# One fifth of the first MLP layer's matmuls on half the TensorE array

## The chip, the cores and the metric

The kernel runs on one core of one Trainium2 chip. A core has TensorE (PE; its weight loads are listed apart as PEld), VectorE (DVE), ScalarE (ACT), GpSimd (POOL), SyncE (SP, which here issues most transfers) and 16 DMA engines. The metric is the device time of one execution in microseconds (us).

## The reference

The input `x` is 8 batches of 4224 rows of 192 features. A causal convolution over 7 rows with softmaxed taps per head comes first; then the real part of a Fourier transform over rows and features is added, each row is normalised, and a two-layer MLP is added to the row:

```python
def _moe_ref(x, w_ch1, w_ch2) -> np.ndarray:
    X = np.fft.fft(x, axis=1)
    X = np.fft.fft(X, axis=2)
    mixed = np.real(X).astype(np.float32)
    u = x + mixed
    ...
    un = (u - mu) / np.sqrt(var + 1e-06)
    ch = np.maximum(un @ w_ch1, 0.0) @ w_ch2
    return (u + ch).astype(np.float32)
```

`w_ch1` is 192 x 768 and `w_ch2` 768 x 192; `x` there is the output of the convolution.

## The kernel before

A batch goes through nine steps: one of 128 tokens (`it == 0`) and eight of 512, so 72 steps in all. Work of four kinds overlaps.

- **Front of later batches**: the convolution (`conv_part`, on TensorE from tile `xt`, and `conv_tap`, on ScalarE and GpSimd from `xg`), a scratch `sc` in memory, loads of `xs` from it (`load_x`, L484), their split in float16 halves `xh` and `xl`, and the transforms `stage_b` (matmuls into `pb`) and `stage_a` (into `pv`, then `V`).
- **`prep`** of the next two steps: matmuls into `pe` (64 array columns wide in iteration 0, 128 otherwise), the residual `u` with `xr`, the normalised rows `un`, and their float16 halves in `hl`. `transposes` turns `hl` into `kt` with one DMA from SyncE's queue.
- **`mlp_hidden`**: six hidden tiles of 128 units. Every float32 factor is carried as a high and a low float16 half. The 192 features take two blocks of array rows: features 0 to 127 fill one (`kt[:, 0]` high, `kt[:, 2]` low), and for features 128 to 191 both halves lie in one block, `kt[:, 1]`, high on partitions 0 to 63 and low on 64 to 127. The weights `W1[:, 0]` and `W1[:, 1]` are the halves of rows 0 to 127; `W1[:, 2]` and `W1[:, 3]` are those of the last 64 rows, laid on both halves of the partitions. Five matmuls of 512 tokens make a hidden tile in one PSUM bank `ph`; ScalarE takes its ReLU to `hh` and VectorE the remainder to `hlo`.
- **`mlp_out`**: for each group of 128 tokens of the step before, 18 matmuls of 192 columns (L724, L727, L730) into `po`, then VectorE adds to `u`, which is stored.

PSUM has eight banks: four with the tag `f` (transforms, `pe`, convolution), two `h` (hidden tiles) and two `o` (`po`). The code writes the units of these kinds in an interleaved order, but each engine's final order is made by a scheduler when the program is built, from the waits and the buffers. Each engine runs its own order strictly, and so does SyncE's queue.

Of the kernel before, what the change touches and what calls it, by code (L numbers as in the profile page):

```python
# [11 lines left out]
F32 = mybir.dt.float32  # L12
I32 = mybir.dt.int32
U32 = mybir.dt.uint32
AF = mybir.ActivationFunctionType
# [21 lines left out]
# From batch NB0 on, the heads from HP on are convolved by segments of SR rows, one a  # L37
# partition.
# [3 lines left out]
# Powers of two that keep the float16 halves of the transform in range.  # L42
# [52 lines left out]
def token_rows():  # L95
    """Row of the result for each (group, partition) of one batch."""
# [23 lines left out]
def kernel(  # L120
# [22 lines left out]
    # ------------------------------------------------------------ constants  # L143
# [37 lines left out]
    # band[h][i, r] = weight of tap k where i + r = 125 - k: rows of a padded vector  # L181
# [12 lines left out]
    # taps[:, h, i] = weight of tap 6 - i of head h on all partitions  # L194
    taps = cp.tile([128, NH, KS], F32, name="taps")

    def pow2_of_norm(parts, n, exponent, name):
        """2^exponent * 2^floor(log2(1 / norm)) on all partitions, where norm^2 is the
        sum of parts[:, :n] over partitions and columns."""
        tot = sb.tile([128, 1], F32, tag="nrm", name=f"tot_{name}", bufs=8)  # L200
        nc.vector.tensor_reduce(tot, parts[:, :n], axis=AX.X, op=ALU.add)
        tag, bufs = ("h", 2) if name[0] == "w" else ("f", 4)
# [26 lines left out]
        # sign and top exponent bit, 7 low exponent bits, 23 leading mantissa bits  # L229
# [4 lines left out]
        # the 29 mantissa bits below, as a float32, to round to nearest  # L234
# [4 lines left out]
        # zero below float32's normal range  # L239
# [98 lines left out]
    def store_rows(bt, xa, r0, cols):  # L338
        """The rows from r0 on, and the first of all once more after the last."""
# [20 lines left out]
    def conv_chunk(bt, ch, tag, xt_slot, xa_slot):  # L360
        """All heads of WC windows."""
# [9 lines left out]
        for h0 in range(0, NH, 3):  # L371
# [3 lines left out]
                bufs=4 if tag == "f" else 2,  # L375
# [22 lines left out]
    def conv_part(bt, part):  # L398
        """One head of WL windows of the heads that the tensor engine convolves."""
# [8 lines left out]
        pc = ps.tile([128, WL, GRP], F32, tag="f", name=f"pc_{b}_{part}", bufs=4)  # L408
# [37 lines left out]
    def store_segments(bt, part):  # L446
        """A third of each segment, or the first segments once more after the last."""
# [15 lines left out]
    # ------------------------------------------------------ transform over b and d3  # L463
    def load_x(bt, ch):
# [6 lines left out]
        # Row 33 a + 128 b of the doubled rows below b1, that less 4224 from there.  # L471
# [31 lines left out]
    def stage_b(bt, t):  # L503
# [6 lines left out]
        pb = ps.tile([128, 512], F32, tag="f", name=f"pb_{b}_{t}", bufs=4)  # L510
# [14 lines left out]
    # -------------------------------------------------------------- transform over a  # L525
    def stage_a(bt, it):
        """V of the one or two q of iteration it."""
# [5 lines left out]
        for h, q in enumerate(qs):  # L533
            pv = ps.tile([128, ND, 2, 64], F32, tag="f", name=f"pv_{b}_{it}_{h}", bufs=4)
# [13 lines left out]
        # Times i where the sine's place holds the alternating sum.  # L548
# [8 lines left out]
    # ------------------------------------- transform over j, residual, LN, transposes  # L557
# [25 lines left out]
    def prep(bt, it):  # L583
# [5 lines left out]
        pe = ps.tile([128, 2, ND, NC], F32, tag="f", name=f"pe_{b}_{it}", bufs=4)  # L589
# [47 lines left out]
        # 1 / sqrt(var + eps), one Newton step after the square root  # L637
# [12 lines left out]
        for g in range(ng):  # L650
# [28 lines left out]
    # --------------------------------------------------------------------- the MLP  # L679
    anchor = [None]  # L680

    def in_turn():
        """No earlier than the latest hidden tile."""
        return tc.issue_after(anchor[0]) if anchor[0] else ExitStack()

    def hidden_units(it):
        """Hidden tiles that share a bank."""
        return ((0, 1, 2), (3, 4, 5)) if it == 0 else ((0,), (1,), (2,), (3,), (4,), (5,))

    def mlp_hidden(bt, it, hts):  # L690
        b = bt.b
        nt = 128 if it == 0 else 512
# [5 lines left out]
        hh, hlo = (h[:, hts[0] : hts[-1] + 1, :nt] for h in bt.h[it])  # L698
# [308 lines left out]
```

## Time and profile before

| | |
|---|---|
| time, median of 3 runs | 1469.61 us (1466.17 to 1475.82) |
| span of the profiled execution | 1470.0 us |
| mean granted clock of TensorE | 0.917 |
| PE busy | 1200.6 us (82%), 11324 matmuls |
| PEld, DVE, ACT, POOL busy | 927.6, 1008.5, 747.5, 671.4 us |
| DMA | 170.68 MB, mean 116 GB/s |

The page gives the profiled execution's span, not a time of its own; it lies beside the median. Matmuls are pipelined: a row's duration runs to the end of its result, and the next starts long before. So what a matmul costs in a series is the distance between two starts in the timeline.

### The profile page before, as it was taken

The numbers are of one execution on the slowest core, as the hardware profiler recorded it, in microseconds if no ns is written. First come the engines' busy times: TensorE is split into PE (matmuls) and PEld (weight loads), VectorE is DVE, ScalarE is ACT, GpSimd is POOL, SyncE is SP. The second block draws the span as 40 slices with busy tenths as digits, with TensorE's granted clock in tenths as the row PEclk, the third lists the DMA queues.
The fourth block names the chain that finished last, engine by engine and source line by source line (L and its number), as shares of the span: only waits on it lengthen the run. The fifth ranks groups of instructions, "written<-read, shape, count | busy, mean of one in ns | idle before, by whom it ended". The sixth has DMA issues, their size and how long they took to land.

```text
span 1470.0 us, 29177 instructions
## 1 busy us (share of the span) xinstructions
PE 1200.6 (82%) x11324; PEld 927.6 (63%) x11324; DVE 1008.5 (69%) x2410; ACT 747.5 (51%) x1400; POOL 671.4 (46%) x708
## 2 busy tenths in 40 slices
PE   4038947997699958999599986999689994999998
PEld 4038635775568736777367764687467772788766
DVE  5424856877586758867597685967588674867773
ACT  4145645645566446654466455664476442434432
POOL 0022444654476436854277544864278542224410
PEclk9568987999899989999799998999799997999999
DMA  8455734465623746437443656227563454423312
GB/s 256 91 133 159 204 78 98 91 151 151 142 61 70 183 138 126 95 105 195 94 101 94 145 160 145 67 63 183 139 132 94 107 106 77 83 55 86 88 44 54
DMA packets 322561, 170.68 MB, mean 116 GB/s; under 512 B 279616, under 2 KB 304696, under 8 KB 322424
## 3 DMA queue, kind: packets, MB, share of 16 engines
q1 hardware_dynamic: 236832, 115.45, 34.4%
q10 hardware_dynamic: 75992, 33.72, 9.2%
q0 software_dynamic: 9600, 19.67, 4.9%
q8 instruction: 88, 1.44, 0.4%
q14 instruction: 49, 0.40, 0.1%
HBM read 84.35 MB, written 58.49 MB: 97 GB/s over the span
## 4 chain that ended last, share of the span: by engine, by line
PE 44%; DVE 18%; SPq 13%; DMA 12%; ACT 5%; issue 4%; ACTq 2%; POOL 1%; another core or an unknown queue 0%; DVEq 0%; POOLq 0%
PE ph L705 16%; SPq L484 10%; PE po L730 5%; PE po L727 5%; PE po L724 5%; DVE un L651 4%; DMA kt<-hl 3%; DVE hlo L710 3%; DMA xt<-in_xv_dram 3%; PE pb L515 2%; PE pb L516 2%; PE pb L514 2%; DMA xs<-sc 2%; DVE xl L497 2%; PE pc L378 2%
## 5 line engine op out<-in xcount | busy, mean ns | idle before, releaser
L705 PE MATMUL ph<-kt,W 128*128 128x512 f16 (+1 forms) x2160 | 510.8, 371 | 91.2 <-DMA kt<-hl 53.9
L709 ACT ACTIVATE hh<-ph 128x512 f16<-128x512 f32 (+1 forms) x400 | 236.3, 591 | 338.8 <-PE ph L705 273.1
L724 PE MATMUL po<-W,hh 128*128 128x192 f16 x1584 | 388.8, 249 | 11.8 <-ACT hh L709 6.1
L710 DVE SCALAR_TENSOR_TENSOR hlo<-ph,hh 128x512 f16<-128x512 f32 (+1 forms) x400 | 269.8, 676 | 182.8 <-ACT hh L709 181.1
L730 PE MATMUL po<-W,hlo 128*128 128x192 f16 x1584 | 386.4, 249 | 3.7 <-DVE hlo L710 3.7
L727 PE MATMUL po<-W,hh 128*128 128x192 f16 x1584 | 388.3, 249 | 0.5 <-issue 0.5
L705 PEld LDWEIGHTS <-W 128*128 128x128 f16 x2160 | 199.1, 101 | 246.0 <-issue 60.0
L569 POOL DMA_INDIRECT xr<-sc,rows_sb x200 | 202.4, 1012 | 284.7 <-DMA rows_sb<-in_rows_dram 96.7
L442 POOL TENSOR_TENSOR pr<-pr,pr 128x792 f32<-128x792 f32 x120 | 233.1, 1943 | 173.6 <-ACT pr L437 168.6
L666 POOL TENSOR_TENSOR hl<-un,hl 128x256 f16<-128x256 f32 (+2 forms) x144 | 128.9, 914 | 155.6 <-ACT hl L664 154.6
L724 PEld LDWEIGHTS <-hh 128*128 128x128 f16 x1584 | 159.7, 101 | 32.1 <-ACT hh L709 8.2
L730 PEld LDWEIGHTS <-hlo 128*128 128x128 f16 x1584 | 157.5, 100 | 34.7 <-DVE hlo L710 4.9
L727 PEld LDWEIGHTS <-hh 128*128 128x128 f16 x1584 | 157.2, 99 | 30.6 <-issue 10.5
L437 ACT ACTIVATE pr<-xg,taps 128x792 f32<-128x792 f32 x168 | 159.2, 959 | 12.1 <-POOL pr L442 11.9
L514 PE MATMUL pb<-c_sb,xh 99*128 99x102 f16 x512 | 127.7, 252 | 3.9 <-ACT xh L494 3.9
L515 PE MATMUL pb<-c_sb,xh 99*128 99x102 f16 x512 | 130.4, 258 | 0.0
L516 PE MATMUL pb<-c_sb,xl 99*128 99x102 f16 x512 | 127.2, 255 | 1.2 <-DVE xl L497 1.2
L497 DVE SCALAR_TENSOR_TENSOR xl<-xs,s_x,xh 99x1024 f16<-99x1024 f32 x64 | 99.8, 1564 | 36.5 <-DMA xs<-sc 28.3
L409 PE MATMUL pc<-xt,band 128*120 128x288 f32 x144 | 52.8, 482 | 70.6 <-DMA xt<-in_xv_dram 70.2
L651 DVE TENSOR_SCALAR un<-u,mv,y 128x192 f32<-128x192 f32 x264 | 103.2, 449 | 9.0 <-POOL hl L666 3.7
L514 PEld LDWEIGHTS <-xh 99*128 99x128 f16 x512 | 103.3, 202 | 7.7 <-ACT xh L494 4.2
L516 PEld LDWEIGHTS <-xl 99*128 99x128 f16 x512 | 105.1, 209 | 2.8 <-DVE xl L497 1.4
(138 smaller groups left out, 2107.4 us busy)
## 6 DMA issues: line engine op xcount, KB each, us to landing
out_dram<-u SPq DMA_DIRECT2D x63, 384.0 KB
sc<-xa ACTq DMA_DIRECT2D x24, 540.0 KB
xg<-in_xg_dram SPq DMA_DIRECT2D x18, 624.0 KB
xt<-in_xv_dram SPq DMA_DIRECT2D x18, 576.0 KB
sc<-xg ACTq DMA_DIRECT2D x18, 528.0 KB
xt<-in_xw_dram SPq DMA_DIRECT2D x12, 576.0 KB
xs<-sc SPq DMA_DIRECT2D x24, 264.0 KB
xr<-sc SPq DMA_DIRECT2D x128, 48.0 KB
```

The costliest lines, as they stand in the source:

```text
L442: nc.gpsimd.tensor_tensor(to, bt.acc, pr, op=ALU.add)
L514: nc.tensor.matmul(po, bt.xh[:, :, j], R[:, 0], start=True, stop=False)
L515: nc.tensor.matmul(po, bt.xh[:, :, j], R[:, 1], start=False, stop=False)
L516: nc.tensor.matmul(po, bt.xl[:, :, j], R[:, 0], start=False, stop=True)
L569: nc.gpsimd.indirect_dma_start(xr[:, g], None, sc[:S], bass.IndirectOffsetOnAxis(ap=rows_sb[:, col : col + 1], axis=0),)
L651: nc.vector.tensor_scalar(un[:, g], u[:, g], mv[:, g, 0:1], y[:, g : g + 1], op0=ALU.subtract, op1=ALU.mult,)
L705: nc.tensor.matmul(ph[:, n], W1[:, w, ht * 128 : (ht + 1) * 128], kt[:, k, :nt], start=(i == 0), stop=(i == len(order) - 1),)
L709: anchor[0] = nc.scalar.activation(hh, ph, AF.Relu).ins
L710: nc.vector.scalar_tensor_tensor(hlo, ph, 0.0, hh, op0=ALU.max, op1=ALU.subtract)
L724: nc.tensor.matmul(po[:, g % 2], hh[:, ht, tk], W2[:, ht, 0], start=(ht == 0), stop=False)
L727: nc.tensor.matmul(po[:, g % 2], hh[:, ht, tk], W2[:, ht, 1], start=False, stop=False)
L730: nc.tensor.matmul(po[:, g % 2], hlo[:, ht, tk], W2[:, ht, 0], start=False, stop=(ht == 5),)
```

## The change

The fifth matmul of a hidden tile multiplied the low halves of the last 64 weight rows by both halves of the tokens. Now it takes only the high halves of the tokens, on 64 array rows. The tokens of a step are cut in two sides of 256, each with a PSUM bank of its own; the first side's matmul uses array rows 0 to 63 and the second side's rows 64 to 127. For that, `prep` swaps the two halves of features 128 to 191 in `hl` for the last two of the four token groups. The other four matmuls use the whole array as before, but on 256 columns, twice. Two hidden tiles share a bank, so three units of two tiles take the place of six units of one. PSUM is dealt out as three banks `f`, three `h` and two `o`. The product of low half by low half of features 128 to 191 is no longer computed. In the 128-token steps there is one side, and the fifth matmul uses rows 0 to 63.

```diff
-        tag, bufs = ("h", 2) if name[0] == "w" else ("f", 4)
+        tag, bufs = ("h", 3) if name[0] == "w" else ("f", 3)
...
+        rest = un[:, :ng, 128:D]
+        if ng == 1:
+            ends = bl[:, 1, :, 0:64], bl[:, 1, :, 64:128]
+        else:
+            rest = rest.rearrange("p (h g) d -> p h g d", h=2)
+            flat = hl.rearrange("p n d -> p (n d)")
+            ends = (
+                flat[:, a : a + 2 * n].rearrange("p (h x d) -> p h x d", h=2, d=64)[
+                    :, :, 0:3:2
+                ]
+                for a, n in ((512, 320), (576, 192))
+            )
         parts = (
             (un[:, :ng, 0:128], bl[:, 0], bl[:, 2]),
-            (un[:, :ng, 128:D], bl[:, 1, :, 0:64], bl[:, 1, :, 64:128]),
+            (rest, *ends),
         )
...
-        return ((0, 1, 2), (3, 4, 5)) if it == 0 else ((0,), (1,), (2,), (3,), (4,), (5,))
+        return ((0, 1, 2), (3, 4, 5)) if it == 0 else ((0, 1), (2, 3), (4, 5))
...
-        order = ((0, 0), (1, 0), (0, 2), (2, 1), (3, 1))
-        ph = ps.tile([128, 512], F32, tag="h", name=f"ph_{b}_{it}_{hts[-1]}", bufs=2)
...
+            sides = []
+            for i in range(2):
+                bank = ps.tile(
+                    [128, 2, 256], F32, tag="h", name=f"ph_{b}_{it}_{hts[-1]}_{i}", bufs=3
+                )
+                at = slice(256 * i, 256 * i + 256)
+                sides.append((bank, at, slice(64 * i, 64 * i + 64)))
         for n, ht in enumerate(hts):
-            for i, (w, k) in enumerate(order):
+            cols = slice(ht * 128, ht * 128 + 128)
+            for i, (w, k) in enumerate(((0, 0), (1, 0), (0, 2), (2, 1))):
+                for bank, at, _ in sides:
+                    nc.tensor.matmul(
+                        bank[:, n], W1[:, w, cols], kt[:, k, at],
+                        start=(i == 0), stop=False,
+                    )
+
+            for bank, at, rows in sides:
                 nc.tensor.matmul(
-                    ph[:, n], W1[:, w, ht * 128 : (ht + 1) * 128], kt[:, k, :nt],
-                    start=(i == 0), stop=(i == len(order) - 1),
+                    bank[:, n], W1[rows, 3, cols], kt[rows, 1, at],
+                    start=False, stop=True,
                 )
```

The scheduler orders the new units anew. On TensorE, a hidden tile of batch 2, step 1 stood like this before (L705 is the hidden layer, and its numbered tile is `ph_2_1_3`):

```order
L409 MATMUL pc_4_2_5935<-xt_4_0_5574,band_103 120x288
L705 LDWEIGHTS W1_374
L705 MATMUL ph_2_1_3_5927<-kt_2_1_5718,W1_374 128x512
L705 LDWEIGHTS W1_374
L705 MATMUL ph_2_1_3_5927<-kt_2_1_5718,W1_374 128x512
```

Now L730 is the hidden layer on the whole array and L736 on half of it; the last figure of the name is the side. Where the code is written with the two sides in turn, the first side of tiles 2 and 3 of the same step stands alone, and other work ahead of the second side:

```order
L730 MATMUL ph_2_1_3_0_6369<-kt_2_1_6198,W1_374 128x256
L736 LDWEIGHTS W1_374
L736 MATMUL ph_2_1_3_0_6369<-kt_2_1_6198,W1_374 128x256
L409 MATMUL pc_4_1_6430<-xt_4_0_6054,band_103 120x288
```

So a half-array matmul stands between whole-array ones there, without its partner. In other units the two sides do stand in turn:

```order
L730 MATMUL ph_2_2_3_1_6618<-kt_2_2_6462,W1_374 128x256
L736 LDWEIGHTS W1_374
L736 MATMUL ph_2_2_3_0_6617<-kt_2_2_6462,W1_374 128x256
L736 LDWEIGHTS W1_374
L736 MATMUL ph_2_2_3_1_6618<-kt_2_2_6462,W1_374 128x256
L595 LDWEIGHTS V_2_4_6169
```

Over the whole order, 183 of the 384 hidden tiles of 512 tokens have their two halves next to each other; for 201 they stand apart. TensorE's matmuls pass from one form of the array (whole, 64 columns, 64 rows) to another 1306 times, and 46 times before.

On SyncE's queue, between two transposes of batch 3, before:

```order
L676 DMA_TRANSPOSE kt_3_2_8252<-hl_3_2_8192 128x12x128
L423 DMA xg_5_8297<-in_xg_dram 128x1248 x3
L484 DMA xs_4_2_8454<-sc_4_5914 17x32x64
L484 DMA xs_4_2_8454<-sc_4_5914 16x32x64
L484 DMA xs_4_2_8454<-sc_4_5914 17x32x64
L396 DMA xt_5_1_8287<-in_xv_dram 128x1152
L484 DMA xs_4_2_8454<-sc_4_5914 16x32x64
L484 DMA xs_4_2_8454<-sc_4_5914 17x32x64
L484 DMA xs_4_2_8454<-sc_4_5914 16x32x64
L564 DMA xr_3_6_8606<-sc_3_3584 64x192 x2
L676 DMA_TRANSPOSE kt_3_3_8482<-hl_3_3_8385 128x12x128
```

and now:

```order
L689 DMA_TRANSPOSE kt_3_2_9032<-hl_3_2_8932 128x12x128
L423 DMA xg_5_9047<-in_xg_dram 128x1248 x3
L484 DMA xs_4_2_9213<-sc_4_6395 17x32x64
L484 DMA xs_4_2_9213<-sc_4_6395 16x32x64
L484 DMA xs_4_2_9213<-sc_4_6395 17x32x64
L484 DMA xs_4_2_9213<-sc_4_6395 16x32x64
L396 DMA xt_5_1_9039<-in_xv_dram 128x1152
L484 DMA xs_4_2_9213<-sc_4_6395 17x32x64
L484 DMA xs_4_2_9213<-sc_4_6395 16x32x64
L564 DMA xr_3_6_9386<-sc_3_3825 64x192 x2
L689 DMA_TRANSPOSE kt_3_3_9277<-hl_3_3_9153 128x12x128
```

The transfers between the two transposes are the same; the load of `xt` has moved behind one more load of `xs`.

More of the change, by code (lines that the diff above doesn't have):

```diff
@@ L374, in conv_chunk @@
                 [128, 3, WC, GRP], F32, tag=tag, name=f"pc_{b}_{ch}_{h0}",
[L375 removed]
+                bufs=3,
             )
@@ L407, in conv_part @@
         cols = slice(h * GRP, (h + 1) * GRP)
-        pc = ps.tile([128, WL, GRP], F32, tag="f", name=f"pc_{b}_{part}", bufs=4)
+        pc = ps.tile([128, WL, GRP], F32, tag="f", name=f"pc_{b}_{part}", bufs=3)
         nc.tensor.matmul(
@@ L588, in prep @@
         ng = 1 if it == 0 else 4
-        pe = ps.tile([128, 2, ND, NC], F32, tag="f", name=f"pe_{b}_{it}", bufs=4)
+        pe = ps.tile([128, 2, ND, NC], F32, tag="f", name=f"pe_{b}_{it}", bufs=3)
         for e in range(2):
@@ L697, in mlp_hidden @@
             )
[L698 removed]
         kt = bt.kt[it]
[L700 to L704 removed]
+        if small:
+            bank = ps.tile([128, 512], F32, tag="h", name=f"ph_{b}_{it}_{hts[-1]}", bufs=3)
+            bank = bank[:, : len(hts) * nt].rearrange("p (h t) -> p h t", t=nt)
+            sides = [(bank, slice(0, nt), slice(0, 64))]
+        else:
+            sides = []
[5 more added lines that the diff above has]
+                sides.append((bank, at, slice(64 * i, 64 * i + 64)))
+        for n, ht in enumerate(hts):
+            cols = slice(ht * 128, ht * 128 + 128)
[6 more added lines that the diff above has]
+            for bank, at, rows in sides:
                 nc.tensor.matmul(
[L706 to L712 removed]
+                    bank[:, n], W1[rows, 3, cols], kt[rows, 1, at],
+                    start=False, stop=True,
+                )
+        for bank, at, _ in sides:
+            hh, hlo = (h[:, hts[0] : hts[-1] + 1, at] for h in bt.h[it])
+            anchor[0] = nc.scalar.activation(hh, bank, AF.Relu).ins
+            nc.vector.scalar_tensor_tensor(
+                hlo, bank, 0.0, hh, op0=ALU.max, op1=ALU.subtract
+            )
     def mlp_out(bt, it, g):
```

12 lines of the change are left out of this document (4 added, 8 removed).

## The prediction, made before the changed kernel ran

> **What bounds the kernel now.** I read the page's head and chain first, then TensorE's waits, then stretches of the span, and last single matmuls.
>
> ```profile
> span 1470.0 us, 29177 instructions
> PE 1200.6 (82%) x11324; PEld 927.6 (63%) x11324; DVE 1008.5 (69%) x2410; ACT 747.5 (51%) x1400; POOL 671.4 (46%) x708
> PE   4038947997699958999599986999689994999998
> PE 44%; DVE 18%; SPq 13%; DMA 12%; ACT 5%; issue 4%; ACTq 2%; POOL 1%; another core or an unknown queue 0%; DVEq 0%; POOLq 0%
> ```
>
> TensorE (PE) leads, and its row of slices says how: behind a thin start of four slices stand runs of 9, broken by one or two low slices about every 172 us, which is one batch. The chain of work that ended last gives PE 44% and the DMA queue of SyncE with its transfers 25%. So there are two regimes, and the waits tell them apart:
>
> ```profile
> PE pc L409 <- DMA xt<-in_xv_dram: 70.2, 6, 15.4
> PE pn_w L204 <- DVE tot_w L201: 62.1, 2, 61.7
> PE ph L705 <- DMA kt<-hl: 53.9, 13, 21.3
> PE ph L705 <- DVE hlo L710: 36.9, 40, 4.7
> PE pc L378 <- DMA band<-line_d: 13.3, 1, 13.3
> PE po L724 <- ACT hh L709: 6.1, 6, 1.8
> PE po L724 <- DVE u L736: 4.7, 2, 4.3
> PE pv L540 <- DVE V L545: 4.5, 1, 4.5
> PE pb L514 <- ACT xh L494: 3.9, 2, 3.3
> PE po L730 <- DVE hlo L710: 3.7, 6, 2.0
> ```
>
> Columns are total us, times, longest. Six waits for `xt` (70.2) and one of 21.3 for `kt` are the low slices: one a batch. L204 and L378 are the start. What is left is short: 36.9 for a bank of `ph`, 53.9 − 21.3 = 32.6 for `kt`, 22.9 in the last five rows.
>
> ```profile
> core 0: us, PE busy (x) PEld busy (x) DVE busy (x) ACT busy (x) POOL busy (x), PEclk, DMA share, GB/s
> 690.00:730.00 40.00, 23.75 (x205) 16.40 (x203) 20.69 (x58) 18.52 (x38) 10.07 (x15) 0.79 0.49 135
> 770.00:860.00 90.00, 87.18 (x872) 68.76 (x869) 66.54 (x166) 51.06 (x99) 55.53 (x58) 1.00 0.50 119
> 1250.00:1420.00 170.00, 168.29 (x1666) 129.53 (x1664) 129.45 (x358) 71.54 (x145) 51.46 (x76) 1.00 0.32 74
> ```
>
> In 770 to 860 PE is busy for 97% and in 1250 to 1420 for 99%, at clock 1.00: what is added to PE there is added to the time. In 690 to 730 it is busy for 59%.
>
> **What the change takes from the streaming.** The full price of a matmul in a row of them is the step from start to start, not its duration:
>
> ```profile
> 699.76 0.25 PE L730 MATMUL po<-W,hlo 128*128 128x192 f16 x1
> ...
> 700.75 0.25 PE L730 MATMUL po<-W,hlo 128*128 128x192 f16 x1
> 700.84 1.24 PE L705 MATMUL ph<-kt,W 128*128 128x512 f16 x5
> 701.91 0.25 PE L730 MATMUL po<-W,hlo 128*128 128x192 f16 x1
> ```
>
> Five 512-column matmuls take 701.91 − 700.84 = 1.07 us, 214 ns each; thirteen 192-column ones, of which the first and the last are shown, take 700.84 − 699.76 = 1.08 us, 83 ns each. So a column costs (214 − 83) / 320 = 0.41 ns, and a 256-column matmul, which the trace before doesn't show, is estimated at 83 + 64 × 0.41 = 109 ns. Twice as many weight loads don't lift that:
>
> ```profile
> 824.18 0.19 PE L596 MATMUL pe<-c_sb,V 128*128 128x65 f16 x1
> 824.21 0.20 PE L597 MATMUL pe<-c_sb,V 128*128 128x65 f16 x1
> 824.25 0.19 PE L595 MATMUL pe<-c_sb,V 128*128 128x65 f16 x1
> ```
>
> These step by 30 to 40 ns with a load for each, so a load of 31 ns or so hides under 109.
>
> Hidden tiles of 512 tokens: 64 steps × 6 = 384. Before: 384 × 5 × 214 ns = 410.9 us. After: the eight full-array matmuls, 384 × 8 × 109 = 334.8 us. The two halves behind them cost 109 + 31 = 140 ns if they stand next to each other and run side by side, the second one load behind the first, and 109 each if something stands between them. In the order of the changed program the two stand next to each other for 183 hidden tiles; for the other 201 they stand apart, as in the row `ph_2_1_3_0` shown with the change. So 183 × 0.140 + 402 × 0.109 = 25.6 + 43.8 = 69.4 us. Sum 404.2: **−6.7 us**. (With no overlap within a pair, 183 × 0.218 = 39.9, and the sum is +7.6.) The 48 hidden tiles of the 128-token steps keep five matmuls of the same width.
>
> **What it adds: switches between the full and the half array.** The trace before has no matmul on half the rows, but it has one on half the columns (`pe` of iteration 0, 64 columns wide), and it shows what going there and back costs:
>
> ```profile
> 813.73 0.25 PE L727 MATMUL po<-W,hh 128*128 128x192 f16 x1
> 813.82 0.25 PE L730 MATMUL po<-W,hlo 128*128 128x192 f16 x1
> 813.99 0.22 PE L595 MATMUL pe<-c_sb,V 128*64 128x65 f16 x1
> 814.04 0.20 PE L596 MATMUL pe<-c_sb,V 128*64 128x65 f16 x1
> 814.17 0.27 PE L540 MATMUL pv<-c_sb,wh 128*128 128x128 f16 x1
> 814.28 0.22 PE L541 MATMUL pv<-c_sb,wh 128*128 128x128 f16 x1
> ```
>
> Into the half array: from L730 to L595 0.17 to 0.18 us where the same L730 otherwise takes 0.08 to 0.09, about 94 ns more. Out: from L596 to L540 0.13 where a 65-column matmul otherwise takes 0.03 to 0.04, about 97 more. I take **95 ns a switch**. The order of the changed program goes from one array form to another 1306 times, the old one 46 times: 183 visits by pairs, 402 + 48 by single halves, two switches each, less a few that meet. 1260 × 95 ns = **+120 us**.
>
> The bounds: nothing, if a half on rows needs no switch; and above, the part of a matmul that is still in the pipe when the next could start:
>
> ```profile
> L705 PE MATMUL ph<-kt,W 128*128 128x512 f16 x1920 | 493.4, 389 | 90.0 <-DMA kt<-hl 52.7 <-DVE hlo L710 36.9 <-issue 0.3
> ```
>
> 389 − 214 = 175 ns, 1260 × 175 = 220 us. I take 95 because the row of the same kind (a part of the array, in this kernel) is the nearest.
>
> The Trainium skill bears on this from both sides. Its page "TensorEngine Tiling (Array Packing)", Key Properties, says that changing the tiling mode, not just the tile within it, drains TensorE; for the 64-column tile the rows above agree (94 and 97 ns), for a 64-row tile no run here shows it yet, and by this rule the sum stands as it is. Its page "TensorE: Matmul & The Clock Gate", Part 3, The mechanism, says that a load overlaps with matmuls in flight where its row group differs; by that rule alone the 120 us would be gone, which is the second rival.
>
> **PE's own sum:** −7 + 120 = +113 us, 1.6 us for each of 72 steps, or +127 without overlap in the pairs.
>
> **What hides some of it.** First, the low slices. These are SyncE's own rows:
>
> ```profile
> 686.50 1.43 SPq L676 DMA_TRANSPOSE kt<-hl  x1
> 687.99 1.84 SPq L423 DMA_DIRECT2D xg<-in_xg_dram  x3
> 689.93 16.12 SPq L484 DMA_DIRECT2D xs<-sc  x3
> 706.16 8.99 SPq L396 DMA_DIRECT2D xt<-in_xv_dram  x1
> 715.19 10.18 SPq L484 DMA_DIRECT2D xs<-sc  x3
> 725.55 1.09 SPq L564 DMA_DIRECT2D xr<-sc  x2
> 726.75 1.41 SPq L676 DMA_TRANSPOSE kt<-hl  x1
> ```
>
> From one transpose to the next the queue spends 40 us on the same twelve issues whatever PE does, and PE has less than 24 us of work for it. In the changed program the same twelve stand between the two transposes (shown with the change); `xt` goes behind a fourth `xs` here, and in another batch ahead of the third. So the wait for `xt` may shrink or turn into a wait for the next `kt`, but this stretch stays, and PE's extra 1.6 us in it are free: seven such stretches, −11 us. Second, the short waits: a slower PE finds evictions and `kt` done. Their sum is 36.9 + 32.6 + 22.9 = 92.4 us; between nothing and all of it I take a third, −31, since the busy stretches (97 and 99%) hold little of it and the waits sit beside the low slices. The third bank of `ph` counts here: with 6 fills a step as before, and three banks for two, the 36.9 are the likeliest to go.
>
> Costed at nothing: the evictions (still 384 of 128x512 on each of ScalarE and VectorE; 595 and 681 ns a piece now, hidden behind PE's matmuls of some 1.2 us a bank). The low halves that go to other places of `hl` keep their element counts. Three banks for the transform instead of four: the waits for it now are the rows L540 and L514, 8.4 us; if that cover goes, twice as much again, +10 to +20, which I keep for the range.
>
> **The sum:** 1470.0 + 113 − 11 − 31 = 1541, rounded to **1540 us**. The profiled execution's span lies 0.4 us over the median of 1469.61, so no correction.
>
> **Rivals.**
> (1) More of it hides: the chain gives PE only 44%, and taken literally 0.44 × 113 = 50 us stay, less some of the bank waits (15): 1505. For it: the chain; against it: the two stretches of 97 and 99%.
> (2) Faster: half a row tile needs no drain, its load being pulled under the matmul ahead. Then the streaming saves 7, and the third bank of `ph` takes about 25 of 36.9 us: 1470 − 30 = 1440. It decides at a switch price of about 25 ns (1260 × 25 = 32 us eats the gain). For it: loads are pulled ahead everywhere in this trace; against it: not once at the 46 switches that it has.
> (3) A row switch waits for the whole pipe, 175 ns: 1470 + 220 − 7 − 42 = 1641. For it: the pair's second half writes another bank; against it: 94 and 97 ns.
> (4) The change doesn't do what it says for the 201 hidden tiles whose halves stand apart. That is in the sum: of the 120 us, 201 × 2 × 95 ns = 38 us come from it.
>
> **Chances and range.** Forecast 0.60 (1515 to 1580), rival 1 0.14 (1480 to 1520), rival 2 0.16 (1425 to 1465), rival 3 0.10 (1590 to 1700). A measurement of this kernel tells 1% from no change, 1455 to 1485. Faster: three quarters of rival 2, 0.12. Within 1%: the rest of it and a quarter of rival 1, 0.08. Slower: 0.80. The range 1450 to 1600 leaves out the lower part of rival 2 and most of rival 3, about 0.18.
>
> **What would show it.** Right: starts of the full-array 128x256 matmuls step by 109 ns, and into and out of the 64-row ones by about 95 more; pairs start about 31 ns apart; waits of L730 for `hlo` well under 37 us; PE busy in most of 1540; the low slice of each batch is still there, on L409 or as a wait for `kt`. Wrong: 64-row matmuls that step by 109 on both sides (rival 2); a step of 280 or more around them (rival 3); or PE's sum as forecast and the span under 1510 (rival 1).

## The result: 5.8% slower, and the profile after

The changed kernel takes 1553.37 us in the median (1551.74 to 1559.72) against 1470.94 for the kernel before on the same chip: ratio 1.0581 [1.0546, 1.0616]. The forecast was 1540 in 1450 to 1600. The number came out, but two parts of its sum were wrong in opposite directions, and that they nearly offset is luck. This shows only when the change is taken apart.

The page of the changed kernel, in the same lines as before:

```profile
span 1557.9 us, 33045 instructions
PE 1315.2 (84%) x13244; PEld 1050.1 (67%) x13244; DVE 1028.2 (66%) x2410; ACT 747.5 (48%) x1400; POOL 670.7 (43%) x708
PE   4057969996899959999689986999689995999999
PE 47%; DVE 16%; SPq 16%; DMA 7%; ACT 4%; issue 4%; POOL 3%; ACTq 2%; another core or an unknown queue 0%; DVEq 0%; POOLq 0%
```

PE is busy for 114.6 us more (1315.2 − 1200.6), the span is 87.9 us longer. The row of slices still has one or two low ones a batch. PE's longest waits (total us, times, longest), with `hlo`'s two:

```profile
PE ph L730 <- DMA kt<-hl: 86.1, 16, 15.8
PE pn_w L204 <- DVE tot_w L201: 60.5, 2, 60.2
PE pc L409 <- DMA xt<-in_xv_dram: 40.7, 5, 13.4
...
PE po L763 <- DVE hlo L743: 11.9, 6, 3.7
...
PE ph L730 <- DVE hlo L743: 4.3, 7, 1.0
```

A ledger helps to read all runs: the span is PE's busy time plus PE's waits. The start (L204, L378) takes some 75 us in every run, so three kinds remain: `kt`, `xt`, and `hlo` (for a bank of `ph` or for `po`), and a rest of small rows. The table sums these waits from PE's rows; with the busy time and the 75 they come within 5 us of the span:

| kernel | PE busy | waits behind the start | kt + xt | hlo |
|---|---|---|---|---|
| before | 1200.6 | 190 | 124.1 | 40.6 |
| after | 1315.2 | 164 | 126.8 | 16.2 |

PE's busy time grew by 114.6, its waits fell by 26 only, and the sum of the waits for transfers did not fall at all.

The tile that a wait is put down to can mislead, so the waits are also sorted by length. Behind the first 150 us, PE has seven waits of over 8 us in either kernel, about one a batch: the low slices. They sum to 102.8 us before and 94.5 after. All shorter waits there sum to 75.2 before and 55.4 after.

PE's own timeline of the changed kernel (start, duration of the group):

```profile
710.82 0.82 PE L730 MATMUL ph<-kt,W 128*128 128x256 f16 x6
711.57 0.28 PE L736 MATMUL ph<-kt,W 64*128 64x256 f16 x2
711.78 1.05 PE L730 MATMUL ph<-kt,W 128*128 128x256 f16 x8
712.76 0.28 PE L736 MATMUL ph<-kt,W 64*128 64x256 f16 x2
```

From 711.78 to 712.76 eight whole-array matmuls take 0.98 us: seven steps of 109 ns and one of some 0.21 into the half array, 0.1 us more than a step. From 711.57 to 711.78 there is another 0.21 us, for both halves and the way out. And the two halves together take 0.28 us, while one such matmul lasts 285 ns on average, by the groups of the same line and shape (busy us and mean ns, then idle time ahead):

```profile
L730 PE MATMUL ph<-kt,W 128*128 128x256 f16 x3072 | 452.5, 280 | 88.1 <-DMA kt<-hl 83.5 <-DVE hlo L743 4.3
L736 PE MATMUL ph<-kt,W 64*128 64x256 f16 x768 | 166.6, 285 | 0.0
```

So the two halves do run side by side; their starts lie 3 ns apart. In single records the step from whole to half array is 205 ns, 96 more than 109, and from half to whole 212, 103 more. PE's sum by these: 1260 switches × 99.5 = +125, less 183 pairs × (109 − 3) = 19, gives 106 above a kernel that has the same matmuls all on the whole array. The first experiment is that kernel.

### The profile page after: what moved, and what is told of

It is laid out like the page before. It is cut to its first block, busy times and chain, and to the rows that moved or that the text cites. A ratio compares the mean times of both kernels' runs of the same rounds, so it can differ in the third digit from the quotient of the medians.

```text
span 1557.9 us, 33045 instructions
## 1 busy us (share of the span) xinstructions
PE 1315.2 (84%) x13244; PEld 1050.1 (67%) x13244; DVE 1028.2 (66%) x2410; ACT 747.5 (48%) x1400; POOL 670.7 (43%) x708
## 4 chain that ended last, share of the span: by engine, by line
PE 47%; DVE 16%; SPq 16%; DMA 7%; ACT 4%; issue 4%; POOL 3%; ACTq 2%; another core or an unknown queue 0%; DVEq 0%; POOLq 0%
PE ph L730 17%; SPq L484 15%; PE ph L736 5%; PE po L757 5%; PE po L763 4%; PE po L760 4%; DMA kt<-hl 4%; DVE un L651 3%; DVE hlo L743 2%; PE pb L514 2%; PE pb L515 2%; PE pb L516 2%; DVE xl L497 1%; ACTq L450 1%; DVE u L624 1%
## 5 line engine op out<-in xcount | busy, mean ns | idle before, releaser
L730 PE MATMUL ph<-kt,W 128*128 128x256 f16 (+1 forms) x3264 | 472.7, 277 | 91.2 <-DMA kt<-hl 86.1
L743 DVE SCALAR_TENSOR_TENSOR hlo<-ph,hh 128x512 f16<-128x512 f32 (+1 forms) x400 | 264.6, 676 | 278.4 <-ACT hh L742 269.0
L763 PE MATMUL po<-W,hlo 128*128 128x192 f16 x1584 | 396.5, 250 | 12.0 <-DVE hlo L743 11.9
L730 PEld LDWEIGHTS <-W 128*128 128x128 f16 x3264 | 285.5, 100 | 167.2 <-issue 79.7
L742 ACT ACTIVATE hh<-ph 128x512 f16<-128x512 f32 (+1 forms) x400 | 224.8, 590 | 358.3 <-PE ph L736 316.1
L757 PE MATMUL po<-W,hh 128*128 128x192 f16 x1584 | 395.9, 250 | 0.2
L760 PE MATMUL po<-W,hh 128*128 128x192 f16 x1584 | 395.0, 250 | 0.0
L736 PE MATMUL ph<-kt,W 64*128 64x256 f16 (+1 forms) x816 | 177.8, 282 | 0.7 <-issue 0.7
L763 PEld LDWEIGHTS <-hlo 128*128 128x128 f16 x1584 | 157.7, 100 | 20.9 <-DVE hlo L743 13.0
L736 PEld LDWEIGHTS <-W 64*128 64x128 f16 x816 | 59.4, 93 | 132.7 <-issue 128.3
L769 DVE SCALAR_TENSOR_TENSOR u<-po,fo,u 128x384 f32<-128x384 f32 (+1 forms) x136 | 80.8, 594 | 83.0 <-PE po L763 70.6
L497 DVE SCALAR_TENSOR_TENSOR xl<-xs,s_x,xh 99x1024 f16<-99x1024 f32 x64 | 88.5, 1402 | 37.5 <-ACT xh L494 37.5
```

Source lines behind the costliest of these rows:

```text
L730: nc.tensor.matmul(bank[:, n], W1[:, w, cols], kt[:, k, at], start=(i == 0), stop=False,)
L736: nc.tensor.matmul(bank[:, n], W1[rows, 3, cols], kt[rows, 1, at], start=False, stop=True,)
L742: anchor[0] = nc.scalar.activation(hh, bank, AF.Relu).ins
L743: nc.vector.scalar_tensor_tensor(hlo, bank, 0.0, hh, op0=ALU.max, op1=ALU.subtract)
L757: nc.tensor.matmul(po[:, g % 2], hh[:, ht, tk], W2[:, ht, 0], start=(ht == 0), stop=False)
L760: nc.tensor.matmul(po[:, g % 2], hh[:, ht, tk], W2[:, ht, 1], start=False, stop=False)
```

## Experiments

My theory: the switches cost PE their price and PE bounds the kernel, so taking the half array away brings the time back to that of before or under it. The rivals: something else in the change costs the time (the order, the banks), or waits take up what PE saves.

### The fifth matmul on the whole array

```diff
-                    bank[:, n], W1[rows, 3, cols], kt[rows, 1, at],
+                    bank[:, n], W1[:, 3, cols], kt[:, 1, at],
```

Each engine's order is that of the changed kernel, row by row.

> The changed kernel with one edit: the fifth matmul of each side takes all 128 array rows again (so the product of low half by low half is back). Every engine's order is the same, instruction for instruction. Theory (switches): the 1262 changes of array form are gone at about 100 ns each, 126 us of PE; the 183 pairs that ran side by side now take 218 instead of 112 ns, 19 us back; PE has about 107 us less, of which 80 to 100% shows: 1450 to 1470 us. Rival (cut columns: twice as many matmuls and loads of half the width are what costs): no change, about 1550. Rival (three banks for the transforms and the new order are what costs): no change, about 1550.

Measured: 1508.12 against 1462.62, ratio 1.0314 [1.0269, 1.0360].

The busy times of the engines on its page:

```profile
PE 1205.9 (80%) x13244; PEld 1118.9 (74%) x13244; DVE 1025.3 (68%) x2410; ACT 741.5 (49%) x1400; POOL 670.6 (45%) x708
```

and PE's longest waits:

```profile
PE ph L730 <- DMA kt<-hl: 96.9, 21, 17.7
...
PE pc L409 <- DMA xt<-in_xv_dram: 51.2, 6, 14.5
PE po L763 <- DVE hlo L743: 23.0, 6, 4.6
PE ph L730 <- DVE hlo L743: 19.5, 28, 1.9
```

Neither the theory nor a rival was met. PE's busy time is 109 us less than in the changed kernel, as the sum above says (106), and the time keeps 3.1% over before, 45 us, with PE only 5 us busier than before. So everything in the change but the half array costs 45 us by the ratio, 34 by the profiled spans (1503.6 − 1470.0); the profile of before is of a run some 9 us longer than the kernel's median beside this run. The half array costs the rest: by the ratios 1.0581 − 1.0314, 39 us, by the spans 54, for 109 us of PE's time. The other half or more was hidden in waits: 219 us behind the start here, 164 in the changed kernel. Against before, the seven long waits are the same (102.0 us), and the shorter ones have grown from 75.2 to 102.5. With three banks `ph`, those for `hlo` are 42.5 us in all, 40.6 before.

### The half array alone, in the order of before

```diff
+                rows = slice(0, 64) if w == 3 else slice(0, 128)
                 nc.tensor.matmul(
-                    ph[:, n], W1[:, w, ht * 128 : (ht + 1) * 128], kt[:, k, :nt],
+                    ph[:, n], W1[rows, w, ht * 128 : (ht + 1) * 128], kt[rows, k, :nt],
```

The fifth 512-column matmul of before takes rows 0 to 63, which leaves out the product of low half by low half. Each engine's order is that of before.

> The kernel before with one edit: the fifth matmul, still 512 columns wide in one bank, takes array rows 0 to 63 alone (which drops the product of low half by low half). Same number of matmuls and columns, same order on every engine. Theory (switches): 910 changes of array form for 46, 864 at about 100 ns are 86 us of PE, of which 65 to 86 us show: 1535 to 1557 us. Rival (cut columns): no change, 1471. Rival (banks and order): no change, 1471.

Measured: 1503.32 against 1462.62, ratio 1.0277 [1.0231, 1.0322].

Its page has

```profile
PE 1275.1 (85%) x11324; PEld 885.5 (59%) x11324; DVE 1010.3 (67%) x2410; ACT 752.8 (50%) x1400; POOL 666.8 (44%) x708
```

and of PE's waits

```profile
PE pc L409 <- DMA xt<-in_xv_dram: 69.1, 5, 14.4
...
PE ph L706 <- DMA kt<-hl: 42.5, 11, 18.4
PE ph L706 <- DVE hlo L711: 15.5, 17, 5.0
```

In its timeline, the five matmuls of one hidden tile and what follows them:

```profile
800.41 1.35 PE L706 MATMUL ph<-kt,W 128*128 128x512 f16 x5
801.69 0.29 PE L514 MATMUL pb<-c_sb,xh 99*128 99x102 f16 x1
```

Five matmuls take 801.69 − 800.41 = 1.28 us instead of 1.07: the two switches, 0.1 us each, at 512 columns as at 256. PE's busy time grows by 74.5 us (the 384 large tiles make 384 × 199 ns = 76; with the 48 small ones there are 864 switches, 86 us, and the clock, below, takes some back), the time by 41. By the profiled spans the time grows by 33, since the waits of PE sum to 42 us less. Nothing was reordered, so the difference is cover: the `hlo` wait for `ph` falls from 36.9 to 15.5, the one for `kt` from 53.9 to 42.5, and the small rows shrink. Most of it is in the waits under 8 us, 75.2 to 38.8; the seven long ones go from 102.8 to 98.2. I had expected 32 to 54 us more of time.

### Twice that price

```diff
+                rows = slice(0, 64) if w in (1, 3) else slice(0, 128)
...
```

The second and the fifth matmul take rows 0 to 63, in the order of before; the second so leaves out features 64 to 127 of its product.

> The kernel before with two of the five matmuls of a hidden tile, the second and the fifth, on array rows 0 to 63 (the second so drops features 64 to 127 of one product, the fifth the product of low half by low half). Same order on every engine as before and as with one half; 1774 changes of array form, 864 more than with one. Theory (PE's short waits hide added time until they are used up; with one half the wait for hlo had fallen from 36.9 to 15.5 us and that for kt from 53.9 to 42.5): of 86 us more on PE, 60 to 85 show: 1563 to 1590 us. Rival (a fixed share near one half shows, as with one half): 40 to 48 us more, 1543 to 1552.

Measured: 1562.26 against 1464.03, ratio 1.0680 [1.0621, 1.0738].

Busy times, from its page:

```profile
PE 1364.7 (87%) x11324; PEld 865.1 (55%) x11324; DVE 1014.5 (65%) x2410; ACT 757.9 (49%) x1400; POOL 668.5 (43%) x708
```

PE's waits:

```profile
PE pc L409 <- DMA xt<-in_xv_dram: 61.3, 5, 13.3
PE ph L706 <- DMA kt<-hl: 32.3, 6, 16.8
...
PE ph L706 <- DVE hlo L711: 5.5, 4, 3.5
```

PE 164 us more, the time 98. The waits give cover of 42 us for the first 75, and 31 more for the next 90: of PE's extra time 55% shows at first and 60% over the whole (44 and 55% by the spans). The short waits are used up first: 17.0 us of 75.2 are left, and 87.5 of the long ones' 102.8. The time lies just under the theory's range (1563 to 1590) and above the rival's (1543 to 1552).

### Three banks for the hidden layer, without anything else

PSUM of before dealt out as in the change, in every allocation of the two tags:

```diff
-        ph = ps.tile([128, 512], F32, tag="h", name=f"ph_{b}_{it}_{hts[-1]}", bufs=2)
+        ph = ps.tile([128, 512], F32, tag="h", name=f"ph_{b}_{it}_{hts[-1]}", bufs=3)
...
-        pe = ps.tile([128, 2, ND, NC], F32, tag="f", name=f"pe_{b}_{it}", bufs=4)
+        pe = ps.tile([128, 2, ND, NC], F32, tag="f", name=f"pe_{b}_{it}", bufs=3)
```

> The kernel before with PSUM dealt out as in the changed kernel: three banks for the transforms and three for the hidden tiles, for four and two. Theory (switches; the third bank takes most of the 36.9 us that TensorE waits for hlo, and the lost transform bank costs up to 10): 1440 to 1460 us. Rival (three banks for the transforms cost): slower than before, 1490 or more.

Measured: 1496.15 against 1462.62, ratio 1.0240 [1.0193, 1.0287]. Of PE's waits:

```profile
PE pc L409 <- DMA xt<-in_xv_dram: 79.5, 7, 16.0
PE ph L705 <- DMA kt<-hl: 74.0, 17, 21.4
...
PE po L730 <- DVE hlo L710: 28.2, 15, 4.7
...
PE ph L705 <- DVE hlo L710: 2.7, 8, 1.1
```

This is the clearest of the misses: I had expected 1440 to 1460, and the time is in the rival's range (1490 or more, by the missing bank of the transforms). The third bank does at its own place what the forecast said: the wait of `ph` for `hlo` falls from 36.9 to 2.7. But the same `hlo` is waited for at `po` now (3.7 before, 28.2 here), so that 10 us of 40.6 are gained, and the waits for `xt` and `kt` grow by 9 and 20. As I read it, PE gets ahead of VectorE by a bank and meets the same tile later. The waits behind the start sum to 222 us, 32 more than before.

### Three banks for the transforms alone, and a third bank taken from `po`

With three `f`, two `h` and two `o` banks, one being left empty (one of six such lines):

```diff
-                bufs=4 if tag == "f" else 2,
+                bufs=3 if tag == "f" else 2,
...
```

> The kernel before with three PSUM banks for the transforms instead of four; two for the hidden tiles as before, one bank unused. The hidden tiles stay spread between the other matmuls in TensorE's order. Theory A (the loss of 2.4% with three and three banks comes from the hidden tiles standing in bursts in the new order, so that hlo and kt come late): within 1% of before, 1455 to 1480 us. Theory B (it comes from the missing transform bank): 2 to 3% slower, 1490 to 1505 us.

Measured: 1483.49 against 1461.22, ratio 1.0156 [1.0130, 1.0182], between theory A (1455 to 1480) and theory B (1490 to 1505). With four `f`, three `h` and one `o` (the lines of `h` are left out here):

```diff
...
-            bt.po[it] = ps.tile([128, 2, D], F32, tag="o", name=f"po_{b}_{it}_{g}", bufs=2)
+            bt.po[it] = ps.tile([128, 2, D], F32, tag="o", name=f"po_{b}_{it}_{g}", bufs=1)
```

> The kernel before with three PSUM banks for the hidden tiles, four for the transforms as before, and one for po instead of two. The hidden tiles stand in bursts of two or three again. Theory A (bursts): 1.5 to 4% slower, 1485 to 1525 us, the bank of po adding to it. Theory B (the missing transform bank): only the bank of po costs, and the third hidden bank gains: 1445 to 1475 us.

Measured: 1478.70 against the same 1461.22, ratio 1.0127 [1.0106, 1.0148], again between the two (1445 to 1475 and 1485 to 1525). Of PE's waits in this second one:

```profile
PE ph L705 <- DMA kt<-hl: 136.9, 21, 20.1
...
PE ph L705 <- DVE hlo L710: 15.4, 11, 4.1
```

Here the wait for `xt` is nearly gone (2.8 us in one wait) and the one for `kt` has become 136.9: their sum is 139.7, 124.1 before. The seven long waits are all put down to `kt` and sum to 100.9 us, 102.8 before: the stretch of transfers on SyncE decides when PE goes on, whichever tile is named. The `hlo` wait falls to less than half, and the time is longer. All three dealings of banks come with a new order, so what a bank does and what the order does can't be read apart here.

### The order alone

No bank, matmul or width is changed; the code writes six hidden units of a step two at a time, as the changed kernel does with its units of two tiles:

```diff
-        hid = [call(mlp_hidden, bt, it, hts) for hts in hidden_units(it)] if bt else []
+        hid = []
+        if bt:
+            units = hidden_units(it)
+            pairs = [units[i : i + 2] for i in range(0, 6, 2)] if it else [(u,) for u in units]
+            for some in pairs:
+                hid.append(lambda some=some: [mlp_hidden(bt, it, hts) for hts in some])
```

> The kernel before with one thing of the change: the code writes the hidden tiles two at a time between the other units of a step (three units instead of six), still one tile of 512 columns a bank, with four, two and two banks. The same matmuls, loads and banks; only the order that the scheduler makes is another. Theory (the 45 us that the full fifth matmul left are the price of another order, whatever made it): 1 to 2.5% slower, 1478 to 1500 us, with PE's busy time unchanged and its waits up by 15 to 35 us. Rival (they are the price of the banks and the cut columns): within 1%, 1450 to 1478 us.

Measured: 1511.51 against 1461.74, ratio 1.0330 [1.0300, 1.0361].

The page's busy times:

```profile
PE 1202.8 (79%) x11324; PEld 923.0 (61%) x11324; DVE 1017.4 (67%) x2410; ACT 753.5 (50%) x1400; POOL 660.3 (44%) x708
```

PE's longest waits:

```profile
PE ph L705 <- DMA kt<-hl: 76.8, 18, 18.8
PE ph L705 <- DVE hlo L710: 70.3, 41, 21.7
...
PE pc L409 <- DMA xt<-in_xv_dram: 50.1, 4, 15.9
```

PE does the same work (1202.8) and the kernel is 50 us slower. Another order by itself costs as much as all of the change but its half array. Theory and rival were both under it. The 70.3 for `hlo` mislead: 21.7 of them are one wait, from 1265 us into the span on, in which VectorE itself stands idle for 20.9 us ahead of that `hlo`. It is the last low slice, where the kernel before waits 21.3 us for `kt`. The seven long waits sum to 107.3 us, and it is the short ones that grew, from 75.2 to 112.9: those for `kt` by 21, for `hlo` by 8, the rest in small rows. So no single wait carries the price.

A second kernel with a new order cuts each 512-column matmul in two of 256 in the same bank, so it also has twice the hidden matmuls and loads:

```diff
+            for at in (slice(0, nt // 2), slice(nt // 2, nt)) if it else (slice(0, nt),):
...
-                    ph[:, n], W1[:, w, ht * 128 : (ht + 1) * 128], kt[:, k, :nt],
+                        ph[:, n, at], W1[:, w, cols], kt[:, k, at],
...
```

> The kernel before with every hidden matmul of 512 columns cut into two of 256, all five for the first 256 columns of the bank and then all five for the last; whole array, banks as before (four, two, two). Theory (a cut costs its streaming alone): 384 x (10 x 109 - 5 x 216) ns = 4 us of PE, and the order is made anew: within 1% of before, 1455 to 1478 us. Rival (twice the matmuls and loads cost of themselves, and are part of the 45 us of the full fifth matmul): 1480 or more.

Measured: 1497.10 against 1464.03, ratio 1.0229 [1.0180, 1.0279]. PE is busy for 1209.4 us, 9 more than before, as the estimate of 109 ns has it (384 × 10 × 109 − 410.9 = +8), and the time grows by 33. That is in the rival's range (1480 or more), which had the matmuls and loads cost of themselves. PE's sum shows 9 us of that; whether the rest is the order or the loads, this run doesn't tell.

### Fewer switches

The changed kernel with the two halves held behind their last whole-array matmul, so that they stand together in all 384 tiles and the switches fall from 1306 to 897:

```diff
-                    nc.tensor.matmul(
+                    last = nc.tensor.matmul(
...
+            with tc.issue_after(last.ins):
+                for bank, at, rows in sides:
```

> The changed kernel, with the two half-array matmuls of a hidden tile held next to each other: the first is queued behind the last whole-array matmul of the second side, for all 384 tiles. Theory (switches): 897 changes of array form for 1306, 409 x 100 ns = 41 us, and 201 more pairs side by side save 106 ns each, 21 us; PE has 62 us less, and with the new order it brings about: 1485 to 1510 us. If the scattered halves cost nothing: 1550. Rival (cut columns; banks): no change, about 1550.

Measured: 1544.42 against 1462.62, ratio 1.0558 [1.0512, 1.0605]. PE is busy for 1261.2 us, 54 less than in the changed kernel, and the ratio is 1.0558 for 1.0581, no difference by their intervals; the rival's "no change, about 1550" is the nearer one. And with the halves of both tiles of a unit together, four in a row, 520 switches:

```diff
...
+            last = whole(0, hts[0], True)
+            with tc.issue_after(last):
+                halves(0, hts[0], False)
+                last = halves(1, hts[1], True)
+            with tc.issue_after(last):
+                whole(1, hts[1], False)
```

> The changed kernel with the halves of both hidden tiles of a unit grouped: eight whole-array matmuls of the first tile, its two halves, the two halves of the second tile first in its sum, then the second's eight. 520 changes of array form for 1306, and all 384 pairs next to each other. Theory (switches and order): 786 x 100 ns and 201 x 106 ns are 100 us of PE less than in the changed kernel, of which 40 to 60% shows, as between the changed kernel and the full fifth matmul: 1490 to 1515 us. If all of it showed: 1453. Rival (only banks and order count): 1540 to 1555, as with the held pairs.

Measured: 1527.11 against 1461.22, ratio 1.0443 [1.0423, 1.0463]. PE is busy for 1233.7 us, 82 less; the ratio is lower by 0.014, about 20 us. Both expectations were too low, by 34 us and 12 us: the first booked most of PE's saving as time and the second 40 to 60% of 100, where the waits behind the start rose from 164 to 202 and 217 us.

### Two banks for the two sides

The changed kernel with four banks `f` and two `h`, so that a unit fills both its banks and the next has none (one of the lines):

```diff
-                    [128, 2, 256], F32, tag="h", name=f"ph_{b}_{it}_{hts[-1]}_{i}", bufs=3
+                    [128, 2, 256], F32, tag="h", name=f"ph_{b}_{it}_{hts[-1]}_{i}", bufs=2
...
```

> The changed kernel with PSUM dealt out as before: four banks for the transforms, two for the hidden tiles. 1523 changes of array form for 1306, 70 pairs for 183: 217 x 100 + 113 x 106 ns are 34 us more PE. Theory A (bursts through the third hidden bank cost): the bursts go, but a unit needs both banks, so units wait for evictions: 1550 to 1600 us. Theory B (missing transform bank): 34 us of PE against 35 to 45 us gained back: about 1550 or less.

Measured: 1600.05 against 1461.22, ratio 1.0962 [1.0938, 1.0986], the slowest kernel of all, at the upper end of theory A's range. Its order has 1523 switches and only 70 pairs, so PE is busy for 1361.8 us, 47 more: 217 × 99.5 = 22 from switches, 113 × 106 = 12 from pairs, and for the rest see the clock under the next run. The waits for `hlo` are 63.5 us (16.2 in the changed kernel), but 32.3 of them are two waits at low slices, and all waits together are 12 us less than in the changed kernel. So by its profile the loss is PE's own, through the switches and lost pairs of the order that two banks bring about.

### No fifth matmul at all

```diff
-        order = ((0, 0), (1, 0), (0, 2), (2, 1), (3, 1))
+        order = ((0, 0), (1, 0), (0, 2), (2, 1))
```

> The kernel before without the fifth matmul of a hidden tile (the low weight halves of the last 64 rows are left out of the sum). 384 x 216 ns = 83 us less PE. Theory (half of a change in PE's sum shows, the rest turns into waits on SyncE's queue and VectorE): 1415 to 1435 us. If all of it showed: 1380. If PE did not bound: 1460. Half of whatever this gains is the most that a free half array could have brought.

Measured: 1466.47 against 1464.03, ratio 1.0040 [0.9998, 1.0083].

Its page's busy times:

```profile
PE 1128.1 (77%) x10892; PEld 889.1 (61%) x10892; DVE 1036.9 (71%) x2410; ACT 749.3 (51%) x1400; POOL 673.0 (46%) x708
```

and PE's waits:

```profile
PE ph L705 <- DMA kt<-hl: 110.7, 16, 19.6
...
PE ph L705 <- DVE hlo L710: 54.9, 43, 2.9
PE po L724 <- DVE u L736: 27.8, 15, 5.6
PE po L730 <- DVE hlo L710: 26.8, 7, 22.8
PE ph L705 <- DMA xs<-sc: 16.0, 1, 16.0
```

PE loses 72.5 us of busy time and gains 68 of waits; the time doesn't move. I had expected 29 to 49 us less; measured is the expectation's last case, 1460 if PE did not bound. A half array that cost nothing at all would have saved no time in an order like this one. Part of it may be the new order's price again (some 18 to 50 us in the runs above, against some 32 to 43 that 44 to 60% of 72.5 would be); the run can't tell the two apart.

PE's busy time is not its work alone, and this run shows it best. In the trace before, a stretch where PE is busy throughout has a granted clock of 0.50 (the column behind the busy times):

```profile
411.50:414.40 2.90, 2.90 (x12) 1.48 (x11) 2.90 (x12) 2.90 (x5) 2.89 (x4) 0.50 0.13 34
```

and in it five 512-column matmuls take 2.14 us, twice their 1.07:

```profile
411.42 2.34 PE L705 MATMUL ph<-kt,W 128*128 128x512 f16 x5
413.56 0.37 PE L724 MATMUL po<-W,hh 128*128 128x192 f16 x1
```

Most such stretches stand at a wait of PE and for some us behind it, and the mean granted clock of a run falls with them: 0.917 before, 0.899 here. By the clock records PE is busy in them for 97 us before and 125 here. At half speed that makes up to 14 us more of busy time for the same work, an estimate, and 85 − 14 is close to the 72.5 that went (384 × 216 ns and 48 small tiles are 85). The same estimate gives 11 us of the 13 that the kernel with two banks left open (103 and 125 us at half clock), and 20 where the grouped halves saved 18 less than the 100 expected (143 us). For the half array alone (70 us) it takes 13 off the 86 of its 864 switches, and 74.5 were measured. So a long wait can cost PE twice: its own length, and a slower clock for some us behind it.

All runs in one table: PE's busy time, the part of it at half clock, and PE's waits behind the first 150 us, over 8 us and under.

| kernel | ratio | PE busy | at clock 0.5 | long waits | short waits |
|---|---|---|---|---|---|
| before | 1 | 1200.6 | 97 | 102.8 | 75.2 |
| after | 1.0581 | 1315.2 | 103 | 94.5 | 55.4 |
| full fifth | 1.0314 | 1205.9 | 105 | 102.0 | 102.5 |
| half alone | 1.0277 | 1275.1 | 70 | 98.2 | 38.8 |
| two halves | 1.0680 | 1364.7 | 74 | 87.5 | 17.0 |
| banks 3, 3, 2 | 1.0240 | 1189.3 | 80 | 116.2 | 91.4 |
| three `f` | 1.0156 | 1194.1 | 75 | 107.3 | 90.4 |
| one `o` | 1.0127 | 1195.6 | 92 | 100.9 | 86.4 |
| order alone | 1.0330 | 1202.8 | 107 | 107.3 | 112.9 |
| cut in two | 1.0229 | 1209.4 | 114 | 94.4 | 101.0 |
| pairs held | 1.0558 | 1261.2 | 119 | 103.4 | 84.1 |
| grouped | 1.0443 | 1233.7 | 143 | 103.7 | 98.6 |
| two `h` | 1.0962 | 1361.8 | 125 | 66.3 | 73.3 |
| no fifth | 1.0040 | 1128.1 | 125 | 128.5 | 117.3 |

The long waits lie within 94 to 116 us in all but three kernels. What an order costs, and what hides PE's added time, are the short ones: every kernel with a new order and no slower PE has 86 to 117 us of them, where before has 75.

No kernel here beats the one before.

## Why the prediction came out, step by step

**Streaming, 256 columns at 109 ns: right.** The step is 109 ns, and the kernel with the whole-array fifth matmul has PE 5.3 us above before, where the same sum gave +7.6 without overlap.

**The pairs: right, with a better overlap.** 3 ns apart and not 31: about 5 us less than forecast.

**The switch at 95 ns: right.** 96 in and 103 out for a tile of 64 rows, measured at both widths. Rivals 2 and 3 (none, and 175 ns) are ruled out. The Trainium skill's page "TensorEngine Tiling (Array Packing)", Key Properties, says that a change of the tiling mode drains TensorE. The runs agree that each change holds the next matmul back, by those numbers; that the array is empty by then they don't show, since the next matmul starts 205 ns behind one whose row lasts 280 on average, and these ends are modelled. The Trainium skill's page "TensorE: Matmul & The Clock Gate", Part 3, The mechanism, says that a load overlaps with matmuls in flight only where its row group differs. The trace agrees between the two halves (3 ns). Where the whole array and half of it meet, the half's 64 rows are among the whole array's, so that rule promises no overlap there, and rival 2 asked more of it than it says.

**PE's sum of +113: right**, +114.6.

**"What is added to PE there is added to the time": wrong.** This is the first of the two terms that failed. I took it from two busy windows (97 and 99%) and let 42 of 113 us be hidden. In the same order, PE's time shows up only in part: 41 of 74.5 us, 98 of 164, and 39 to 54 of 109; the short waits hide the rest, until they are used up. So 55 to 70 us of the 109 are hidden. Rival 1, the chain's 44% taken literally, gives 0.44 × 109 = 48 and described this term better than the forecast. The measured shares (36 to 60%) lie around it; they move with the waits that are left, so 44% is no constant.

**"The third bank of `ph` counts here" (of the −31) and three transform banks at nothing: wrong.** This is the second. The wait of `ph` for `hlo` went as said, 36.9 to 4.3, and came back in part: `po` for `hlo` (3.7 to 11.9) and short waits for `kt` (19 to 28). With the half array taken out, the third bank gained nothing: 42.5 us of waits for `hlo` and 40.6 before. There the change's new order, banks and cut columns cost +45 us by the ratios (34 by the spans), where the forecast had 8 for PE less some part of the 31. I had priced each edit, and not the order that the scheduler makes anew from them. That another order alone is worth this much is shown (+3.3%); that the 45 are the order's is likely by it and not shown, and which property of an order makes it slow, or makes that of before good, is not settled.

The two together: the half array cost 39 us and the rest 45 by the ratios, 54 and 34 by the spans, 84 to 88 in all. The forecast had 105 of PE's 113 less the 11 for the half array, 8 for the rest, and the −31, which it argued from a slower PE and from the third bank at once. Put wholly to the half array, that makes 63 and +8; put wholly to the rest, 94 and −23. Either way the half array was forecast too dear, by 9 to 55 us, and the rest too cheap, by 26 to 68. Their sum of 71 is near the measured one, and 1540 within 1% of 1553, by luck: two errors that have nothing to do with each other.

**The low slices, −11: right, nearly in size too.** SyncE's rows of the changed kernel from one transpose to the next:

```profile
715.89 1.43 SPq L689 DMA_TRANSPOSE kt<-hl  x1
717.37 1.82 SPq L423 DMA_DIRECT2D xg<-in_xg_dram  x3
719.29 25.24 SPq L484 DMA_DIRECT2D xs<-sc  x4
744.64 0.42 SPq L396 DMA_DIRECT2D xt<-in_xv_dram  x1
745.11 10.55 SPq L484 DMA_DIRECT2D xs<-sc  x2
755.83 1.09 SPq L564 DMA_DIRECT2D xr<-sc  x2
757.03 1.43 SPq L689 DMA_TRANSPOSE kt<-hl  x1
```

The same twelve issues take 41.1 us (40.3 before). A wait for `xt` turned into one for `kt`, as said: 70.2 + 53.9 before, 40.7 + 86.1 now. That sum grew by 2.7, but it mixes the low slices with short waits for `kt`. The seven long waits alone fell from 102.8 to 94.5, by 8 of the 11 forecast, and by 7.5 between the whole-array kernel and the changed one, in one order (102.0 to 94.5).

**Evictions at nothing: right as far as seen.** The wait of `po` or `ph` for `hlo` is 16 us in all, less than before.

**Rival 4** (halves apart) is in the sum and has its price: with all pairs held together PE saves 54 us, though the time doesn't.

## What to carry to other kernels

A use of part of the array can pay only if many such matmuls follow one another: here each way in or out costs 0.1 us, as much as the matmul it saves. No kernel here shows it paying; with four halves in a row PE is still busy for 28 us more than on the whole array (1233.7 and 1205.9). To price an engine's added time, read the chain's share and the short waits beside the busy windows, and test it by a run in the same order: here 36 to 60% of it showed, and time taken from the same engine came back as waits. Sort waits by length and place before reading them by tile. And a bank or unit changed in code whose order a scheduler makes is a change of the whole order: before pricing the edit, price that, by a run that changes the order alone (here 3.3%).

## What the runs showed of the hardware

Two 64-row matmuls on different halves of the array, into two banks, start 3 ns apart and, by the modelled ends, end 3 ns apart too. A switch costs the same within 10 ns for a tile of 64 rows (96 in, 103 out) as for one of 64 columns (94 and 97), and the same behind 256 and 512 columns (96 and 103 at both), so it isn't a share of the matmul's length. At a granted clock of 0.50 a step takes twice as long as at 1.00: 427 and 216 ns for 512 columns, 213 and 109 for 256.
